# First feed-forward set: lot 5's raw weights in the spare lower-x slot, a lot's rounding ahead of the last lot's lower part, lower weights' products last

## The chip, the cores and the metric

One core of a Trainium2 chip runs the kernel. The metric is the device time of one execution in microseconds (us), lower is better; a measurement is the median of several runs. TensorE (PE), VectorE (DVE), ScalarE (ACT) and GpSimd (POOL) each run their own instruction queue in order; SyncE (SP) issues most DMAs, in order too. They wait for one another by semaphores.

## The reference

Decayed linear attention in blocks, and then a feed-forward layer with squared ReLU, all in float32:

```python
# q, k, v: (4, 8, 768, 64), lam: (8,)
for b in range(S // 64):
    intra = einsum('bhic,bhjc->bhij', qb, kb) * Dmask      # lam ** (i - j), i >= j
    out_b = einsum('bhij,bhjd->bhid', intra, vb) + einsum('bhid,bhde->bhie', qb * lam_pow, kv_state)
    kv_state = lam_block * kv_state + einsum('bhsd,bhse->bhde', kb * rev_pow, vb)
x = out.transpose(0, 2, 1, 3).reshape(3072, 512)
h = maximum(x @ w_in, 0)                                    # w_in: (512, 2048)
y = (h * h) @ w_out                                         # w_out: (2048, 512)
```

## The kernel before

The 3072 tokens are 24 chunks of 128; four chunks make a set of 512 tokens (`N`), and there are six sets. Each float32 product on PE is made as three products of rounded operands: an upper part (`h`) and a lower part (`l`, what the rounding left) of each side, upper by upper, lower by upper, upper by lower. So the weights must stand in SBUF as `wh` and `wl`, and a set's attention result as `xh` and `xl`.

The change lies in the loop over the first set, `for f in range(NF)` at line 1075, 16 iterations. Iteration f computes `hidden(0, f)` (12 matmuls: 128 columns of `w_in`, upper and lower weights, by 512 tokens), squares it on ACT (`square`, three instructions), takes the lower part `gl` on DVE (`rest`), and runs `project(0, f - 1)` (12 matmuls into four accumulators). Beside that, every fourth iteration carries one chunk of attention of the next set: `step = f % 4` tells which piece (scores in step 0, masked scores and the scaled query in step 1, `attend` in step 2, state and lower x in step 3).

The same loop prepares the weights. They are given in float64 and read as pairs of 32-bit words, in 17 lots (`NLOT`); lot u holds block u of `w_in` and block u - 1 of `w_out`, and iteration f needs lot f complete. A lot goes through these steps:

- `wload(u)`: SP issues two DMAs of 512 KB into a tile `raw` (tag "raw", two slots). It is called two iterations ahead of the lot's rounding, and waits until the slot is free.
- `first_hi(u)`, line 120, and `first_lo(u)`, line 125: two ACT passes over `raw`; the first writes a new tile `A` (tag "A", two slots), the second works in place in `raw`.
- `clamp`, `shift`, `sign`, lines 133, 137, 144: three DVE passes over `A`.
- `rounded(u)`, line 150: DVE adds the low word; the last reader of `raw[u]`, whose slot then comes free.
- `upper(u)`, line 156: ACT casts `A` to `wh`.
- `lower(u)`, line 159: DVE writes `A - wh` to `wl`; the last reader of `A`, whose slot then comes free.
- `turn(u)`, line 164: a one-element POOL copy that reads `wl` into `mark`, so that POOL goes on only after `lower`.

In iteration f, `u_ = f + 2`: for f of 3 and more DVE runs clamp, shift and sign of lot u_, then lower of lot u_ - 1, (in step 3 a state update,) then rounded of lot u_, then `gl`. ACT runs first_hi and first_lo of lot u_ + 1 behind the squares, and the cast of lot u_ - 1 ahead of them (in step 2 that of lot u_ behind the passes). POOL runs, behind `turn`, the fading of the state (`fade_state`, line 508) and the scaling of keys (`scale_k`, line 382) in step 0, and of the query (`scale_q`, line 390) in step 1. Iterations 0 to 2 have orders of their own.

The tag "xl" has two slots of the same size as a `raw` tile. One holds the first set's lower x; the other held chunk 3's lent attention operands, whose last reader runs before the loop, and is kept for the second set's lower x, which `attend` starts to write in step 3 of the first four iterations (line 367). A tag's new tile takes a slot that is free in the order of the program. The schedule is by hand: the order of the calls is the order of each queue.

Of the kernel before, what the change touches and what calls it, by code (L numbers as in the profile page):

```python
# [7 lines left out]
F32 = mybir.dt.float32  # L8
F32R = mybir.dt.float32r
U32 = mybir.dt.uint32  # L10
I64 = mybir.dt.int64
AF = mybir.ActivationFunctionType
ALU = mybir.AluOpType
PSUM = bass.MemoryType.PSUM

P = 128
# [5 lines left out]
DM = H * D  # L22
DF = 2048
KT = DM // P
NF = DF // P
G = 4
N = G * C
# [4 lines left out]
NLOT = NF + 1  # L32
# [3 lines left out]
def body(ctx: ExitStack, tc: tile.TileContext, qT, kT, kvq, lam, w, out):  # L36
# [3 lines left out]
    wk = ctx.enter_context(tc.tile_pool(name="wk", bufs=2))  # L40
# [53 lines left out]
    wh = const.tile([P, 2 * NF, DM], F32R, name="wh")  # L94
    wl = const.tile([P, 2 * NF, DM], F32R, name="wl")
# [4 lines left out]
    def lot(t, u):  # L100
        if u in (0, NF):
            return t[:, u : u + 1]
        return t.rearrange("p (s f) d -> p s f d", s=2)[:, :, u]

    def pieces(u):
        return [x for x in ((0, u), (1, u - 1)) if 0 <= x[1] < NF]

    raw, cv = {}, {}

    def wload(u, engine=nc.sync):  # L110
        if u < NLOT:
            x = pieces(u)
            raw[u] = wk.tile([P, len(x) * DM], I64, name="raw", tag="raw")
            for i, (side, f) in enumerate(x):
                engine.dma_start(out=raw[u][:, i * DM : (i + 1) * DM], in_=w[side, :, f])

# [31 lines left out]
    def rounded(u):  # L148
        L, Hw, A = cv[u]
        V.tensor_tensor(out=A, in0=A, in1=L, op=ALU.add)  # L150

    def whole(u):
        return cv[u][2].bitcast(F32).rearrange("p (a d) -> p a d", d=DM)

    def upper(u):
        nc.scalar.copy(lot(wh, u), whole(u))  # L156

    def lower(u):
        V.tensor_tensor(out=lot(wl, u), in0=whole(u), in1=lot(wh, u).bitcast(F32), op=ALU.subtract)  # L159
        cv.pop(u)  # L160
# [15 lines left out]
    def where(x, base, pattern, step, compare, fill):  # L176
# [17 lines left out]
        out=pz[:, C - T : C - T + NX], data0=s[:, 0:1].broadcast_to([P, NX]), data1=spike,  # L194
# [13 lines left out]
    for j in range(2):  # L208
# [5 lines left out]
        lambda o, x, y, op=op: V.tensor_tensor(out=o, in0=x, in1=y, op=op)  # L214
# [5 lines left out]
    b_, t_, u_, c_, d_, af = (sq[:, i, 0 : NS - 1] for i in range(6))  # L220
# [11 lines left out]
    for k in range(NS - 3, NS):  # L232
        n = 1 << k
        V.tensor_scalar(
            out=pz[:, Z + n : Z + 2 * n], in0=pz[:, Z : Z + n], scalar1=tr[:, k : k + 1], scalar2=None,
# [42 lines left out]
    xs_of = {}  # L278
# [81 lines left out]
    def attend(t):  # L360
        KEPT[t] = wk.tile([P, DM], F32, name="kept", tag="a")
        go(t, t + 1, False, scored=False)
        xh, xl = xs_of[t // G]
        cs = slice(t % G * C, (t % G + 1) * C)
        x = KEPT.pop(t).rearrange("p (a b) -> p a b", a=KT)
        nc.scalar.copy(xh[:, :, cs], x)
        return lambda: V.tensor_tensor(
            out=xl[:, :, cs], in0=x, in1=xh[:, :, cs].bitcast(F32), op=ALU.subtract
        )

    part_of = {}
# [71 lines left out]
    def begin(t):  # L443
        begun_of[t] = [ps_a.tile([P, DM], F32, name="att") for _ in range(2)], set()
        old_state(t, 0)

    def begun_mark(t):
        c = (NPR - 1) * D
        nc.scalar.copy(mark[:, 2:3], begun_of[t][0][0][0:1, c : c + 1])

    def go(t, after, apart, mid=None, scored=True):
        if t not in begun_of:
            begin(t)
            begun_mark(t)
        o = u = begun_of[t][0]
        vs = tok[t][1]
        if after is not None and scored:
            scores_by_half(after, ps_h, "h")
            if apart:
                u = sc_of[after]  # L460

        def all_news():
            for p in range(NPR):
                if t % NCB < NCB - 1:
                    news_of(0, t, u[0], p, apart)
                if after is not None:
                    news_of(1, after, u[1], p, apart)

        if apart:
            all_news()  # L470
        old_state(t, 1)
        a = a_of.pop(t)
        for p in range(NPR):
            for h in range(2):
                for j, r in enumerate(rows):
                    add_to(t, h, p, j, vs[rows[h], 2 * p + j, :], a[rows[h], j, p, :], True)
        if not apart:
            all_news()
        if after is not None:
            part_of[after] = u[1]  # L480
            if scored:
                masked_by_half(after)
        if mid is not None:
            mid()
        x = kept(t).rearrange("p (a two c) -> p a two c", two=2, c=C)
        for h in range(2):
            y = o[h][:, 0 : NPR * D].rearrange("p (a two c) -> p a two c", two=2, c=D)
            nc.scalar.copy(x[:, :, 0, of_half(h)], y[:, :, 0])
            for j, r in enumerate(rows):
                nc.scalar.copy(x[r, :, 1, of_half(h)], y[rows[1 - j], :, 1])  # L490
        part_of[t] = u[0]
# [22 lines left out]
    def hidden(m, f, xh, xl):  # L514
        h = ps_h.tile([P, N], F32, name="h")
        k = 0
        for wt, x in ((wh, xh), (wl, xh), (wh, xl)):
            for kt in range(KT):
                nc.tensor.matmul(  # L519
                    h, wt[:, f, kt * P : (kt + 1) * P], x[:, kt], start=k == 0, stop=k == 11  # L520
                )
                k += 1
        return h

    def square(h):
        nc.scalar.activation(h, h, AF.Relu)  # L526
        gh = wk.tile([P, N], F32R, name="gh")
        nc.scalar.activation(gh, h, AF.Square)
        nc.scalar.activation(h, h, AF.Square)  # L529
        return gh  # L530
# [38 lines left out]
                for k in range(i, i + n):  # L569
                    step(k)  # L570

    def new_x(m):
        xs_of[m] = [wk.tile([P, KT, N], F32R, name=n, tag=n) for n in ("xh", "xl")]

# [111 lines left out]
    wt = dram.tile([NF // 2, P, 4, 2, 2 * P], F32, name="wt")  # L688
# [320 lines left out]
    o, u, low = {}, {}, {}  # L1009
# [61 lines left out]
    scale_k(G)  # L1071

    prev = None
    new_x(1)
    for f in range(NF):
        t, step, u_ = G + f // 4, f % 4, f + 2
        h = hidden(0, f, *xs_of[0])
        if step == 2:
            begin(t)
        if f == 2:  # L1080
            gh = square(h)
            begun_mark(t)
            upper(u_ - 1)
        if f < 3:
            if f < 2:
                lower(u_ - 1)
            clamp(u_)
            shift(u_)
            if f == 2:
                lower(u_ - 1)  # L1090
            if f == 1:
                turn(u_, True)
                masked_by_half(t)
                scale_q(t)
                scale_k(t + 1)
                state(t, True)
            sign(u_)
            if f != 1:
                rounded(u_)
        else:  # L1100
            if u_ < NLOT:
                for op in (clamp, shift, sign):
                    op(u_)
            if step < 3:
                upper(u_ - 1)
            lower(u_ - 1)
            if u_ - 1 < NF:
                turn(u_ - 1, False)
            if step == 3:
                state(t, False)  # L1110
            if u_ < NLOT:
                rounded(u_)
        wload(u_ + 2)
        if f == 0:
            fade_state(False)
        if step == 0 and f:
            if t % NCB < NCB - 1:
                fade_state(True)
            scale_k(t + 1)
        if step == 1 and f > 1:  # L1120
            scale_q(t)
        if f != 2:
            gh = square(h)
            if step == 2:
                begun_mark(t)
        rest(0, f, h, gh)
        if step == 3:
            low[t]()
            state(t + 1, True, f == NF - 1)
        if f == 1:  # L1130
            rounded(u_)
        if step == 1 and f > 1:
            masked_by_half(t)
        if f == 0:
            upper(u_)
        if u_ + 1 < NLOT:
            first_hi(u_ + 1)
            first_lo(u_ + 1)
        if step == 2 and u_ < NLOT:
            upper(u_)  # L1140
        if prev is not None:
            project(*prev)
        prev = (0, f)
        if step == 2:
            low[t] = attend(t)
            load_qk(t + 2)
            load_kv(t + 2)
        if f == 0:
            open_half(t)
        elif step == 0:  # L1150
            scores_by_half(t, ps_a, "att")
        if f == NF - 1:
            scores_by_half(t + 1, ps_a, "att")
            scale_k(t + 2)
# [14 lines left out]
    for j, tag in enumerate(("xh", "xl")):  # L1169
        x = wk.tile([P, 4, DM], F32, name="raws", tag=tag)  # L1170
# [14 lines left out]
    for f in range(NF):  # L1185
        t = first_t + f // 2
# [16 lines left out]
        if f == NF - 1:  # L1203
            x = far(*pair(3))
# [4 lines left out]
        if f % 2 == 0:  # L1209
            go(t, t + 1 if t < last_t else None, False)  # L1210
            if t == last_t:
                x = near(*pair(3), "a")
# [16 lines left out]
    m, first_t, last_t = 2, 4 * G, 6 * G - 1  # L1229
# [11 lines left out]
    for f in range(NF):  # L1241
        t = first_t + f // 2
# [97 lines left out]
```

## Time and profile before

| | us |
|---|---|
| median of 3 runs | 585.36 (584.14 to 586.4) |
| the profiled execution | 585.99 |
| its span in the trace | 584.3 |
| PE busy | 572.0 (98%) |
| DVE busy | 415.5 (71%) |
| ACT busy | 278.6 (48%) |
| POOL busy | 101.6 (17%) |

All times below are us from the span's start, in that one execution; the loop over the first set takes from 25.5 to about 124. "Busy" counts instructions only, not waiting. Matmuls are pipelined: one of 512 columns is shown with some 0.39 us, and they follow one another every 0.227. A wait's view tells who waited for whom, and in a timeline a bracket at the end of a line tells how long the engine stood idle just before, and whose end it awaited. The granted TensorE clock is 1.00 in the whole loop.

### The profile page before, as it was taken

To read this page: it belongs to the slowest core of one execution; us is meant where nothing else is said; L and a number is where in the kernel's file an instruction comes from. 1 tells how busy PE (TensorE), PEld (TensorE's weight loads), DVE (VectorE), ACT (ScalarE), POOL (GpSimd) and SP (SyncE) were. 2 spreads that over 40 slices of the span, in tenths; PEclk is the share of its full clock that TensorE was granted. 3 is DMA by queue.
4 is the path that set the end of the run, shared out by engine and by line. 5 is a ranking of instruction groups with operands and counts; after the bars stand their busy time and mean duration, and the time that the engine had idled before them with its cause. 6 is when DMAs were issued, how large, how long until landed. Compare 5 with 4: busy or idle time off the path is not lost.

```text
span 584.3 us, 13118 instructions
## 1 busy us (share of the span) xinstructions
PE 572.0 (98%) x5276; PEld 481.7 (82%) x5276; DVE 415.5 (71%) x685; ACT 278.6 (48%) x529; POOL 101.6 (17%) x110
## 2 busy tenths in 40 slices
PE   9998999999999999999999999999999999999996
PEld 7886787878888887888888887888788888999996
DVE  6898999952678675786666668677645456997933
ACT  4677888844454455433333334445523244641510
POOL 4531322332322231000000003355100000000000
PEclk9999999999999999999999999999999999999999
DMA  8956475424689786466666644632297665767863
GB/s 301 346 170 231 148 256 197 157 75 145 196 277 382 236 272 225 153 191 218 198 199 198 197 163 152 235 124 74 74 315 229 195 194 176 257 213 206 285 204 108
DMA packets 69388, 119.35 MB, mean 204 GB/s; under 512 B 6352, under 2 KB 30928, under 8 KB 69328
## 3 DMA queue, kind: packets, MB, share of 16 engines
q1 hardware_dynamic: 66864, 115.37, 60.7%
q10 hardware_dynamic: 2464, 3.15, 1.5%
q8 instruction: 42, 0.69, 0.4%
q14 instruction: 18, 0.15, 0.1%
HBM read 88.08 MB, written 29.36 MB: 201 GB/s over the span
## 4 chain that ended last, share of the span: by engine, by line
PE 69%; DVE 10%; DMA 9%; ACT 5%; issue 4%; SPq 2%; POOL 1%; DVEq 0%; ACTq 0%; POOLq 0%
PE h L679 19%; PE acc L927 8%; PE att L679 7%; PE acc L549 7%; PE acc L554 6%; PE acc L550 6%; PE h L519 5%; PE att L927 4%; DMA raw<-in_w 3%; PE att L429 2%; PE h L927 2%; DMA kv_sb<-in_kvq 2%; DVE A L144 2%; DMA ws<-parts 2%; DMA lent<-in_qT 1%
## 5 line engine op out<-in xcount | busy, mean ns | idle before, releaser
L549 PE MATMUL acc<-wh,gh 128*128 128x512 f32 x256 | 101.2, 395 | 0.0
L554 PE MATMUL acc<-wh,gl 128*128 128x512 f32 x256 | 100.0, 390 | 0.1
L550 PE MATMUL acc<-wl,gh 128*128 128x512 f32 x256 | 99.7, 389 | 0.0
L679 PE MATMUL h<-wh,ring 128*128 128x512 f32 x320 | 85.8, 390 | 0.1
L526 ACT ACTIVATE h<-h 128x512 f32<-128x512 f32 x48 | 27.9, 582 | 94.8 <-PE h L519 37.0
L679 PEld LDWEIGHTS h<-wh,ring 128*128 128x128 f32 x320 | 59.9, 188 | 13.2 <-issue 0.5
L534 DVE TENSOR_TENSOR gl<-h,gh 128x512 fp32r<-128x512 f32 x48 | 33.0, 688 | 40.1 <-ACT h L529 40.1
L554 PEld LDWEIGHTS acc<-wh,gl 128*128 128x128 f32 x256 | 48.0, 188 | 11.0 <-DVE gl L534 0.9
L549 PEld LDWEIGHTS acc<-wh,gh 128*128 128x128 f32 x256 | 48.0, 188 | 10.4
L550 PEld LDWEIGHTS acc<-wl,gh 128*128 128x128 f32 x256 | 48.1, 188 | 9.7
L679 PE MATMUL h<-wl,ring 128*128 128x512 f32 x160 | 49.3, 389 | 0.0
L508 POOL TENSOR_TENSOR kvd<-kv,qpow 128x256 f32<-128x256 f32 x33 | 28.9, 874 | 85.2 <-DVE kv L214 74.5
L382 POOL TENSOR_TENSOR kv_sb<-kv_sb,mask 128x512 f32<-128x512 f32 x17 | 20.9, 1227 | 125.1 <-DMA kv_sb<-in_kvq 123.4
L519 PE MATMUL h<-xh,wh 128*128 128x512 f32 x128 | 36.7, 408 | 1.4 <-ACT wh L156 1.0
L519 PE MATMUL h<-xh,wl 128*128 128x512 f32 x128 | 34.8, 394 | 1.1 <-DVE wl L159 1.0
L927 PE MATMUL acc<-folds,wh 128*128 128x256 f32 x192 | 35.2, 283 | 0.0
L679 PEld LDWEIGHTS h<-wl,ring 128*128 128x128 f32 x160 | 30.0, 188 | 6.3
L519 PE MATMUL h<-xl,wh 128*128 128x512 f32 x128 | 34.3, 390 | 0.0
L679 PE MATMUL att<-wh,ring 128*128 128x512 f32 x128 | 34.2, 389 | 0.0
L214 DVE TENSOR_TENSOR wl<-sums,wh 128x1024 fp32r<-128x1024 f32 x24 | 29.3, 1219 | 1.8 <-ACT wh L899 1.8
L519 PEld LDWEIGHTS h<-xh,wl 128*128 128x128 f32 x128 | 23.8, 188 | 7.5 <-DVE wl L159 2.4
L927 PEld LDWEIGHTS acc<-folds,wh 128*128 128x128 f32 x192 | 30.0, 192 | 0.0
(249 smaller groups left out, 1189.6 us busy)
## 6 DMA issues: line engine op xcount, KB each, us to landing
ring<-ws SPq DMA_DIRECT2D x112, 256.0 KB, 3.0
folds<-wt SPq DMA_DIRECT2D x64, 256.0 KB, 3.7
raw<-in_w SPq DMA_DIRECT2D x30, 512.0 KB, 4.4
kv_sb<-in_kvq SPq DMA_DIRECT2D x19, 512.0 KB, 5.5
ws<-parts SPq DMA_DIRECT2D x32, 256.0 KB, 4.7
qk_sb<-in_kT SPq DMA_DIRECT2D x20, 256.0 KB, 4.6
qk_sb<-in_qT SPq DMA_DIRECT2D x20, 256.0 KB, 4.5
out_x<-o SPq DMA_DIRECT2D x16, 256.0 KB, 4.7
```

The costliest lines, as they stand in the source:

```text
L144: V.scalar_tensor_tensor(out=A, in0=Hw, scalar=0xC0000000, in1=A, op0=ALU.bitwise_and, op1=ALU.bitwise_or)
L214: lambda o, x, y, op=op: V.tensor_tensor(out=o, in0=x, in1=y, op=op)
L382: nc.gpsimd.tensor_tensor(out=x, in0=x, in1=y.broadcast_to([P, NPR, 2, D]), op=ALU.mult)
L508: nc.gpsimd.tensor_tensor(out=kvd, in0=d, in1=qpow[:, :, D - 1 : D].broadcast_to([P, NPR, D]), op=ALU.mult)
L519: nc.tensor.matmul(h, wt[:, f, kt * P : (kt + 1) * P], x[:, kt], start=k == 0, stop=k == 11)
L526: nc.scalar.activation(h, h, AF.Relu)
L534: V.tensor_tensor(out=gl, in0=r, in1=gh.bitcast(F32), op=ALU.subtract)
L549: nc.tensor.matmul(accs[m][i], gh[:, cs], wh[:, j], start=f == 0, stop=False)
L550: nc.tensor.matmul(accs[m][i], gh[:, cs], wl[:, j], start=False, stop=False)
L554: nc.tensor.matmul(accs[m][i], gl[:, cs], wh[:, j], start=False, stop=end)
L679: nc.tensor.matmul(bank, x[:, part_, kt], t[:, q + kt], start=start and z == 0, stop=stop and z == 5, skip_group_check=True,)
L927: nc.tensor.matmul(bank[:, r * 2 * P : (r + 1) * 2 * P], x, y, start=n == 0 and r == 0 and z == 0, stop=n == NQ - 1 and z == 2, skip_group ...
```

## The change

`wload` takes lot 5's tile from the tag "xl" and not from "raw". The second set's lower x is therefore made later: `new_x(1, False)` makes the upper one alone, and `new_low(1)` the lower one in iteration 3, behind the rounding of lot 5; `attend` looks the lower tile up only when it writes. From iteration 3 on, `rounded(u_)` is called right behind `sign(u_)`, ahead of `lower(u_ - 1)`, `turn` and the state update. In `hidden` of the first set, for f of 1 and more, the four products of the lower weights come last, behind those of the lower x.

```diff
@@ -110,7 +110,7 @@
     def wload(u, engine=nc.sync):
         if u < NLOT:
             x = pieces(u)
-            raw[u] = wk.tile([P, len(x) * DM], I64, name="raw", tag="raw")
+            raw[u] = wk.tile([P, len(x) * DM], I64, name="raw", tag="xl" if u == G + 1 else "raw")
             for i, (side, f) in enumerate(x):
                 engine.dma_start(out=raw[u][:, i * DM : (i + 1) * DM], in_=w[side, :, f])
 
@@ -360,12 +360,12 @@
     def attend(t):
         KEPT[t] = wk.tile([P, DM], F32, name="kept", tag="a")
         go(t, t + 1, False, scored=False)
-        xh, xl = xs_of[t // G]
+        xh = xs_of[t // G][0]
         cs = slice(t % G * C, (t % G + 1) * C)
         x = KEPT.pop(t).rearrange("p (a b) -> p a b", a=KT)
         nc.scalar.copy(xh[:, :, cs], x)
         return lambda: V.tensor_tensor(
-            out=xl[:, :, cs], in0=x, in1=xh[:, :, cs].bitcast(F32), op=ALU.subtract
+            out=xs_of[t // G][1][:, :, cs], in0=x, in1=xh[:, :, cs].bitcast(F32), op=ALU.subtract
         )
 
     part_of = {}
@@ -514,7 +514,10 @@
     def hidden(m, f, xh, xl):
         h = ps_h.tile([P, N], F32, name="h")
         k = 0
-        for wt, x in ((wh, xh), (wl, xh), (wh, xl)):
+        order = ((wh, xh), (wl, xh), (wh, xl))
+        if m == 0 and f:
+            order = order[0], order[2], order[1]
+        for wt, x in order:
             for kt in range(KT):
                 nc.tensor.matmul(
                     h, wt[:, f, kt * P : (kt + 1) * P], x[:, kt], start=k == 0, stop=k == 11
@@ -569,8 +572,11 @@
                 for k in range(i, i + n):
                     step(k)
 
-    def new_x(m):
-        xs_of[m] = [wk.tile([P, KT, N], F32R, name=n, tag=n) for n in ("xh", "xl")]
+    def new_x(m, low=True):
+        xs_of[m] = [wk.tile([P, KT, N], F32R, name=n, tag=n) for n in ("xh", "xl")[: 1 + low]]
+
+    def new_low(m):
+        xs_of[m].append(wk.tile([P, KT, N], F32R, name="xl", tag="xl"))
 
 
 
@@ -1071,7 +1077,7 @@
     scale_k(G)
 
     prev = None
-    new_x(1)
+    new_x(1, False)
     for f in range(NF):
         t, step, u_ = G + f // 4, f % 4, f + 2
         h = hidden(0, f, *xs_of[0])
@@ -1103,13 +1109,15 @@
                     op(u_)
             if step < 3:
                 upper(u_ - 1)
+            if u_ < NLOT:
+                rounded(u_)
+            if f == 3:
+                new_low(1)
             lower(u_ - 1)
             if u_ - 1 < NF:
                 turn(u_ - 1, False)
             if step == 3:
                 state(t, False)
-            if u_ < NLOT:
-                rounded(u_)
         wload(u_ + 2)
         if f == 0:
             fade_state(False)
```

## Rows read from the trace of the kernel before

**Rows 1.** Busy time: length; PE, PEld, DVE, ACT, POOL; clock, DMA share, GB/s.

```profile
60.00:80.00 20.00, 19.58 (x157) 15.43 (x156) 19.32 (x24) 16.84 (x27) 5.26 (x5) 1.00 0.67 218
```

**Rows 2.** Waits of PE, 24 to 125: waiter, releaser, us, times, longest.

```profile
PE h L519 <- DVE wl L159: 1.0, 2, 0.7
PE h L519 <- ACT wh L156: 1.0, 1, 1.0
PE att L429 <- ACT mark L449: 0.5, 1, 0.5
PE att L429 <- POOL qk_sb L390: 0.3, 1, 0.3
```

**Rows 3.** Timeline of ACT: start, us, line, operation, tiles, count, [idle before, releaser].

```profile
46.39 1.14 ACT L120 ACTIVATE A<-raw 128x1024 f32<-128x1024 f32 x1 [4.68 <-DMA raw<-in_w]
48.48 1.03 ACT L156 CAST wh<-A 128x1024 fp32r<-128x1024 f32 x1
```

**Rows 4.** Timeline of PE: hidden(0,4), its first and its lower weights' products.

```profile
49.55 1.21 PE L519 MATMUL h<-xh,wh 128*128 128x512 f32 x4 [0.97 <-ACT wh L156]
51.43 1.19 PE L519 MATMUL h<-xh,wl 128*128 128x512 f32 x4 [0.66 <-DVE wl L159]
```

**Rows 5.** Timeline of DVE: lower(3), sign(4), rounded(4), lower(4).

```profile
41.75 1.23 DVE L159 TENSOR_TENSOR wl<-A,wh 128x1024 fp32r<-128x1024 f32 x1
42.89 1.22 DVE L144 SCALAR_TENSOR_TENSOR A<-raw,A 128x1024 uint32<-128x1024 uint32 x1
44.14 1.23 DVE L150 CUSTOM_DVE_ANT_0 A<-raw,A 128x2048 uint16<-128x2048 uint16 x1
...
50.16 1.22 DVE L159 TENSOR_TENSOR wl<-A,wh 128x1024 fp32r<-128x1024 f32 x1
```

**Rows 6.** SP at line 115, 31.5 to 32.5 (lot 4): issues, landing.

```profile
L115 SPq DMA_DIRECT2D raw<-in_w x2: 328/377/426, 31.8 to 32.2; - x2
DMA to landing us min/median/max: 3.7/4.2/4.6
```

**Rows 7.** The same, 45.7 to 46.3 (lot 6; q, k, v behind): landing.

```profile
DMA to landing us min/median/max: 3.8/4.2/4.6
```

**Rows 8.** Timeline of DVE in iteration 6: clamp, sign, lower, rounding, gl.

```profile
66.86 0.69 DVE L133 TENSOR_SCALAR A<-A 128x1024 f32<-128x1024 f32 x1
...
68.31 1.23 DVE L144 SCALAR_TENSOR_TENSOR A<-raw,A 128x1024 uint32<-128x1024 uint32 x1
69.45 1.22 DVE L159 TENSOR_TENSOR wl<-A,wh 128x1024 fp32r<-128x1024 f32 x1
70.59 1.22 DVE L150 CUSTOM_DVE_ANT_0 A<-raw,A 128x2048 uint16<-128x2048 uint16 x1
71.72 0.69 DVE L534 TENSOR_TENSOR gl<-h,gh 128x512 fp32r<-128x512 f32 x1
```

**Rows 9.** Waits of ACT from 24 to 125, its first passes.

```profile
ACT A L120 <- DMA raw<-in_w: 10.6, 7, 4.7
ACT A L120 <- DVE wl L159: 4.0, 4, 1.4
```

**Rows 10.** Timeline of POOL: marks at line 164, and a scaling of keys.

```profile
51.51 0.17 POOL L164 COPY mark<-wl 1x1 f32<-1x1 f32 x1 [10.98 <-DVE wl L159]
...
64.68 1.04 POOL L164 COPY mark<-wl 1x1 f32<-1x1 f32 x1 [3.81 <-DVE wl L159]
...
110.21 1.05 POOL L382 TENSOR_TENSOR kv_sb<-kv_sb,mask 128x512 f32<-128x512 f32 x1
```

**Rows 11.** Timeline of DVE: the clamp of lot 15.

```profile
110.15 1.67 DVE L133 TENSOR_SCALAR A<-A 128x1024 f32<-128x1024 f32 x1
```

**Rows 12.** Timeline of PE: first products of hidden(0,9), (0,10), (0,13).

```profile
83.43 1.19 PE L519 MATMUL h<-xh,wh 128*128 128x512 f32 x4
...
89.00 1.08 PE L519 MATMUL h<-xh,wh 128*128 128x512 f32 x4
...
108.81 1.19 PE L519 MATMUL h<-xh,wh 128*128 128x512 f32 x4
```

## The prediction

> **What bounds the kernel now.** I read the busy time of each engine by stretch first, then the waits of TensorE (PE), then those of ScalarE (ACT), then the timelines around the largest wait. In the loop that the change touches (25 to 122 us; after it PE again has no large waits) PE is busy in nearly all of each stretch, and VectorE (DVE) almost as much [rows 1]: 19.6 and 19.3 of 20 us. PE sets the pace and DVE is just behind it. All that PE visibly waits for in the loop comes to 2.8 us: 1.0 for an upper weight part, 1.0 for lower parts, 0.5 for the mark, 0.3 for the scaled query [rows 2]. The view counts a wait from a modelled end, about 0.16 us after the next matmul could have started, and short gaps around these add a little; so some 4.3 us is all that can be won here, 0.7% of the time.
>
> The largest waits are lot 5's. ACT stands 4.68 us for its raw weights and starts on them at 46.39; only behind its two passes, at 48.48, comes the cast of lot 4's upper part [rows 3]. So PE starts hidden(0,4) at 49.55 after a wait, and stands again until lot 4's lower part is there, at 51.43 [rows 4]. DVE writes that lower part from 50.16 [rows 5].
>
> **Part 1: lot 5's raw weights in the empty lower x.** Before, lot 5 has the slot of lot 3, which comes free when lot 3 is rounded, near 40. The spare xl slot last held chunk 3's lent operands, whose last matmuls run before the loop. So SP, which issues lot 4 at 31.8 and 32.2 [rows 6], issues lot 5 right behind, at about 33. Lot 4 took up to 4.6 us to land; lot 5, with that megabyte ahead of it, should land at 38 to 40 and not at 46.3. This takes no instruction away. Does it hold up lot 4? Lot 6 was issued with a chunk's q, k and v (1 MB as well) right behind on the same queue, and landed in 3.8 and 4.6 us [rows 7], as lot 4 did with nothing behind it: cost 0. The Trainium skill, "DMA: Bandwidth & Descriptors", section "Issuing engines are not separate DMA queues", says that DMAs share the same 16 engines and interleave. Read as sharing between neighbours this would make lot 4 late; [rows 6, 7] do not show that, and I keep it as rival C.
>
> SP is moved too: lots 6 and 7 now take the slots of lots 3 and 4 and are issued one iteration earlier, and chunk 6's loads, queued behind lot 6, go out near 43 instead of 46. Nobody waits for those; value 0.
>
> What is next? The rounding buffer A has two slots, so lot 5's first pass needs lot 3's lower part written; DVE starts that at 41.75 and it takes 1.23 [rows 5]. So ACT runs the passes of lot 5 from 43.0 to 45.3, and the upper cast of lot 4 when lot 4 is rounded (44.14 + 1.23 = 45.4 [rows 5]), ready at 46.4 and not 49.5. hidden(0,4) then starts when PE is free, 1.1 us earlier. DVE need not wait for lot 5 any more and comes to clamp(5) at 45.9 (rounding 1.14 and gl 0.60 behind 44.14). After clamp, shift, sign and rounding (clamp and shift 1.45 and rounding 1.14, from starts in [rows 8]; sign 1.25, from 42.89 to 44.14 in [rows 5], since the rounding right behind must await its result: 0.1 more than before a lower) it reaches lot 4's lower part at 49.7 and ends it at 50.9. Thanks to part 3 PE needs it only 8 matmuls into hidden(0,4), at about 50.3: it waits 0.7, less than the 0.97 that now passes there. With the small gaps behind it PE is 2.0 us ahead at hidden(0,5).
>
> **Part 2: rounding ahead of the lower part.** Per iteration from f = 3 on, rounding (1.14 by starts) moves ahead of lower. It frees the raw slot 1.14 us earlier, and the upper cast can run earlier, but lower(u-1) is 1.2 us later, and three things hang on it.
>
> First, PE's lower weights: paid back by part 3 with 4 matmuls, 0.91 us. Second, the POOL mark and, queued behind it, the query and key scaling. The mark took 1.04 us beside a rounding and 0.17 beside another instruction (64.68 and 51.51) [rows 10]; it now falls beside gl, so POOL gets back 0.9 of the 1.2. Third, and dearest, ACT's first pass of lot u+1: it takes the A slot that lower(u-1) frees, and already waits for just that in 4 iterations, 4.0 us in all [rows 9]. The pass takes 1.14 [rows 3]. Today DVE meanwhile rounds (1.14) and makes gl (0.60) [rows 8], and finds the pass done. After the change it has gl alone. In a plain iteration (steps 0 and 2) DVE's round becomes clamp and shift 1.45 + sign 1.25 + rounding 1.14 + lower 1.22 + pass 1.14 and 0.08 for two handovers (0.03 of it seen between 42.89 + 1.22 and 44.14 in [rows 5]) = 6.28, against 5.46 today (66.86 to 71.72, plus 0.60) and 5.57 that PE takes (83.43 to 89.00 [rows 12]). In step 1 the masked scores (some 0.7) fill the hole, also 6.28. In step 3 low and state fill it: about 6.9, plus some 0.5 of waiting for ACT's squares. Four iterations: 3 x 6.28 + 7.4 = 26.2. In f = 8 and f = 12 POOL's fading and scaling now run right behind the mark, and the clamp comes while they hold the port: a clamp beside such an instruction took 1.67 [rows 11] and not 0.69 [rows 8], and ended 0.56 after POOL's (110.21 + 1.05 [rows 10]). POOL ends at lower + 1.9 and the clamp thus at lower + 2.45 and not 1.9: 0.5 more, 26.7 in all. PE took 25.38 from 83.43 to 108.81 [rows 12]. So DVE, with the A slots, becomes the pace: +1.3 per four iterations.
>
> **Part 3: lower weights' products last.** No instruction more or less; the lower x of set 0 is complete before f = 1. It moves PE's need of the lower weights by 0.91 us. Counted above.
>
> **The sum.** Lead at hidden(0,5): -2.0. Cycle f = 5 to 8: this one has no fading at f = 4, starts with the lead, and today already runs slow for DVE's sake: +0.4 (waits of about 0.65, 0.8 and 0.6 at the lower parts of 5 and 6 and at the query, for 0.6, 0.25 and 0.5). Cycle 9 to 12: +1.3, most at the lower part of lot 10. f = 13 and 14: the plain iterations 12 and 14 and the port again, +1.4, most at the lower part of lot 14. Together +1.1. Other end: the small gaps of today's loop, about 0.1 at each change of tile shape, lie under the new waits or beside them; if beside, up to +2.3. I take +1.5, nearer the end that is counted from the trace's own starts. PE is the pace after the loop, so it reaches the end whole. The profiled execution took 585.99 us (span 584.3, the rest lies around it), 0.6 above the median 585.36, inside the runs' spread. 585.99 + 1.5 = 587.5; against the median, 586.9.
>
> **The rivals.**
> A, forecast: the A slots eat the lead and a little more, 585.4 to 588.5. Chance 0.50.
> B, the lead stays: if PE's gaps rather than DVE set the rounds, or ACT's pass lies under gl and the late clamp costs PE nothing, -2.0 to -2.6 remain: 582.5 to 583.5; the most, with all 4.3 won, 581. For it: today DVE has about 1 us spare in four iterations, and 10.6 us of ACT's waits are for loads that now come earlier [rows 9]. Against it: 6.28 against 5.57. Chance 0.20.
> C, lot 5's load slows lot 4's: by [rows 6, 7] not; if lot 4 lands 1.2 later, ACT's mark comes 1.2 later, of which about 0.5 is slack, and PE stands 0.7 more: 587.6. Chance 0.05. The Trainium skill's sentence on interleaving is this case.
> D, slower: the mechanism of the forecast with the port. If POOL holds the port at the clamp in most iterations, and not only at f = 8 and 12, such an iteration costs 0.5 more and none catches up: four of them beyond the counted ones, 2.0, make +3.5 with the forecast's 1.5: 588.9. It decides from the point at which POOL is still busy when the clamp may start, 1.2 us behind lower, in steps 1 and 2 too. Chance 0.20.
> E, it does not do what it says: lot 5 still starts its passes after 46 (another holder of the slot or of A): no lead, but the price of part 2: about +3.1 (1.1 and the lead of 2.0), 588.5. The slot's last user is long done, which speaks against it; chance 0.05.
>
> **How the numbers follow.** The forecast is A: 586.9. 583.0 to 589.2 leaves out part of B at the low end and the tails of D and E, under 0.2. About 0.5% (2.9 us) is what a measurement of this kernel tells from no change: faster than 582.4 is only the better half of B, 0.10; slower than 588.3 is D, most of E and little of A, 0.23; the rest 0.67.
>
> **What would show it.** Lot 5's first pass at about 43 and PE's wait at hidden(0,4)'s upper part gone (part 1); the POOL mark at about 0.2 us in most iterations; ACT's first pass waiting for the lower part in nearly every iteration and not for a DMA; DVE idle about 0.6 to 0.7 before the clamps of lots 7, 9, 11, 13 and 15; PE waiting about 1.2 for the lower parts of lots 10 and 14 (part 2). If those clamps start without a wait, my round of 6.28 is wrong and it is B.

## The result

The changed kernel took 588.99 us (median of 4 runs, 588.7 to 589.49) against 585.12 of before in the same session: ratio 1.0066, 95% interval [1.0045, 1.0087], 3.9 us slower. Its profiled execution took 589.0 (span 587.3), that of before 585.99 (584.3): 3.0 between the two, since the profiled run of before lay 0.9 above its median. With four runs on each side the interval is wide: 2.6 to 5.1 us slower. In the larger groups timed later, before took 585.95 and 585.76, so the true distance may be nearer 3 than 4.

Where in the loop it went shows in the starts of `hidden(0, f)` on PE. Of the changed kernel (from `hidden` on, line numbers shift by 3; its matmuls are at line 522), from two stretches of PE's timeline (start, us, line, operation, tiles):

```profile
48.33 1.07 PE L522 MATMUL h<-xh,wh 128*128 128x512 f32 x4
...
55.46 1.19 PE L522 MATMUL h<-xh,wh 128*128 128x512 f32 x4
...
82.38 1.19 PE L522 MATMUL h<-xh,wh 128*128 128x512 f32 x4
```

```profile
109.47 1.19 PE L522 MATMUL h<-xh,wh 128*128 128x512 f32 x4
...
124.87 1.19 PE L522 MATMUL h<-xh,wh 128*128 128x512 f32 x4
```

Of before, the two that [rows 4, 12] do not have:

```profile
57.20 1.19 PE L519 MATMUL h<-xh,wh 128*128 128x512 f32 x4
...
122.10 1.19 PE L519 MATMUL h<-xh,wh 128*128 128x512 f32 x4
```

| hidden(0, f) starts | f = 4 | f = 5 | f = 9 | f = 13 | f = 15 |
|---|---|---|---|---|---|
| before | 49.55 | 57.20 | 83.43 | 108.81 | 122.10 |
| after | 48.33 | 55.46 | 82.38 | 109.47 | 124.87 |
| difference | -1.22 | -1.74 | -1.05 | +0.66 | +2.77 |

So the lead of part 1 is there, 1.74 us at f = 5, and is lost again at a growing rate: +0.69 over four iterations, +1.71 over the next four, +2.11 over the last two. From there the distance stays: at the second set's last blocks, near 230 us, it is still 2.74.

The lead first. ACT's first passes over lots 4 and 5 in the changed kernel, DVE's lower part of lot 3, and SP's four issues of lots 4 and 5 with their landings; the last line is the landing of lot 4's two alone:

```profile
36.52 1.14 ACT L120 ACTIVATE A<-raw 128x1024 f32<-128x1024 f32 x1
...
42.93 1.15 ACT L120 ACTIVATE A<-raw 128x1024 f32<-128x1024 f32 x1 [1.61 <-issue]
```

```profile
41.63 1.22 DVE L159 TENSOR_TENSOR wl<-A,wh 128x1024 fp32r<-128x1024 f32 x1
```

```profile
L115 SPq DMA_DIRECT2D raw<-in_w x4: 328/401/430, 31.7 to 33.1; - x4
DMA to landing us min/median/max: 3.4/5.1/6.8
```

```profile
DMA to landing us min/median/max: 3.4/3.9/4.3
```

The pass over lot 5 starts at 42.93 where [rows 3] had 46.39; the load is there by 40 (issued until 33.1, landing within 6.8), and what the pass now waits for is lot 3's lower part, as reckoned. The bracket names no releaser, but the lower part ends at 42.85 (41.63 + 1.22), 0.08 ahead of the pass. PE's wait for lot 4's upper part is gone. What replaced it is PE's new list of waits in the loop, 24 to 128 us (waiter, releaser, us in total, times, longest), and that of ACT's first pass, both to be held against [rows 2, 9]:

```profile
PE h L522 <- DVE wl L159: 4.3, 6, 1.2
PE att L429 <- POOL qk_sb L390: 0.7, 2, 0.4
PE att L429 <- ACT mark L449: 0.3, 1, 0.3
```

```profile
ACT A L120 <- DVE wl L159: 16.9, 9, 2.3
```

```profile
DVE A L133 <- ACT A L120: 3.0, 5, 0.6
```

PE waits 4.3 us for lower weights, not 1.0. ACT's first pass waits for the lower part in 9 iterations, 16.9 us, and no longer for any load; and DVE, which is to clamp what that pass writes, stands 5 times for it. DVE's timeline in iterations 5 to 7 shows the mechanism (a bracket at the end is the idle time before and its releaser):

```profile
59.16 0.70 DVE L133 TENSOR_SCALAR A<-A 128x1024 f32<-128x1024 f32 x1 [0.62 <-ACT A L120]
59.88 0.69 DVE L137 TENSOR_SCALAR A<-A 128x1024 uint32<-128x1024 uint32 x1
60.61 1.23 DVE L144 SCALAR_TENSOR_TENSOR A<-raw,A 128x1024 uint32<-128x1024 uint32 x1
61.98 1.23 DVE L150 CUSTOM_DVE_ANT_0 A<-raw,A 128x2048 uint16<-128x2048 uint16 x1
63.12 1.22 DVE L159 TENSOR_TENSOR wl<-A,wh 128x1024 fp32r<-128x1024 f32 x1
64.25 0.68 DVE L537 TENSOR_TENSOR gl<-h,gh 128x512 fp32r<-128x512 f32 x1
64.86 0.74 DVE L214 TENSOR_TENSOR a<-att,mask 128x256 f32<-128x256 f32 x2
65.55 0.90 DVE L133 TENSOR_SCALAR A<-A 128x1024 f32<-128x1024 f32 x1
...
67.22 1.23 DVE L144 SCALAR_TENSOR_TENSOR A<-raw,A 128x1024 uint32<-128x1024 uint32 x1
68.58 1.23 DVE L150 CUSTOM_DVE_ANT_0 A<-raw,A 128x2048 uint16<-128x2048 uint16 x1
69.72 1.22 DVE L159 TENSOR_TENSOR wl<-A,wh 128x1024 fp32r<-128x1024 f32 x1
70.86 0.68 DVE L537 TENSOR_TENSOR gl<-h,gh 128x512 fp32r<-128x512 f32 x1
72.14 0.69 DVE L133 TENSOR_SCALAR A<-A 128x1024 f32<-128x1024 f32 x1 [0.60 <-ACT A L120]
```

and ACT's pass between the last two:

```profile
70.97 1.14 ACT L120 ACTIVATE A<-raw 128x1024 f32<-128x1024 f32 x1 [1.79 <-DVE wl L159]
```

Lines 133, 137, 144 are clamp, shift and sign, 150 the rounding, 159 the lower part, 537 `gl`. Set it beside [rows 8]: lower now starts behind the rounding (69.72), `gl` follows, and then DVE stands 0.60 us until ACT's pass over the next lot, which could start only when lower ended (69.72 + 1.22 = 70.94), is through. From clamp to clamp iteration 6 takes 6.59 us (65.55 to 72.14), 5.46 before; 0.2 of it is the longer clamp at 65.55. Iteration 5, with masked scores behind `gl`, takes 6.39. A second, smaller cost stands in the same lines: from sign to the next instruction it is 1.36 to 1.37 (60.61 to 61.98, 67.22 to 68.58), where with lower behind sign it was 1.14 (68.31 to 69.45 in [rows 8]). So in every iteration in which it is moved the rounding costs DVE 0.23 us more, and where `gl` alone stands behind lower the hole of 0.6 comes on top.

### The profile page after: what moved, and what is told of

Same layout as the page of the kernel before. It is cut to its first block, busy times and chain, and to the rows that moved or that the text cites. A ratio compares the mean times of both kernels' runs of the same rounds, so it can differ in the third digit from the quotient of the medians.

```text
span 587.3 us, 13123 instructions
## 1 busy us (share of the span) xinstructions
PE 573.3 (98%) x5276; PEld 482.1 (82%) x5276; DVE 416.7 (71%) x685; ACT 278.5 (47%) x529; POOL 93.4 (16%) x110
## 4 chain that ended last, share of the span: by engine, by line
PE 71%; DVE 14%; ACT 6%; issue 4%; DMA 3%; SPq 1%; POOL 0%; DVEq 0%; ACTq 0%; POOLq 0%
PE h L685 19%; PE acc L933 7%; PE att L685 7%; PE acc L552 6%; PE acc L557 6%; PE acc L553 6%; PE h L522 5%; PE att L933 4%; PE att L429 2%; DVE A L144 2%; PE h L933 2%; DVE wl L159 2%; DMA ws<-parts 2%; DVE A L133 1%; DVE sums L214 1%
## 5 line engine op out<-in xcount | busy, mean ns | idle before, releaser
L508 POOL TENSOR_TENSOR kvd<-kv,qpow 128x256 f32<-128x256 f32 x33 | 27.0, 819 | 85.0 <-DVE kv L214 68.0
```

What stands on the lines that cost most here:

```text
L508: nc.gpsimd.tensor_tensor(out=kvd, in0=d, in1=qpow[:, :, D - 1 : D].broadcast_to([P, NPR, D]), op=ALU.mult)
```

## The experiments

Two theories. **A-slot**: rounding ahead of lower puts ACT's first pass into DVE's own round, because the pass needs the A slot that lower frees; DVE's round grows past PE's. **Lateness**: the round matters little, the lower weights simply come 1.2 us later in it, and PE stands for them. They agree on nearly everything in the trace of the change, so each run touches what only one of them cares for. Times are medians; before was timed beside each group of kernels (585.12 beside the change, 585.95 beside the first four below it, 585.76 beside the last three), and the ratios are what is compared.

| kernel | us | ratio to before, 95% interval | us to before |
|---|---|---|---|
| the change | 588.99 | 1.0066 [1.0045, 1.0087] | +3.9 |
| slot_order: rounding put back | 583.43 | 0.9955 [0.9942, 0.9968] | -2.6 |
| round_alone | 590.52 | 1.0078 [1.0066, 1.0090] | +4.6 |
| slot_round: without part 3 | 589.18 | 1.0058 [1.0046, 1.0070] | +3.4 |
| halves | 587.24 | 1.0026 [1.0015, 1.0037] | +1.5 |
| round_odd | 584.59 | 0.9979 [0.9966, 0.9992] | -1.2 |
| round_even | 587.49 | 1.0032 [1.0021, 1.0043] | +1.9 |
| slot_alone | 584.03 | 0.9973 [0.9963, 0.9984] | -1.6 |

(The last column is the ratio times 585.9, less that.)

**slot_order**, the change with one part undone:

```diff
-            if u_ < NLOT:
-                rounded(u_)
-            if f == 3:
-                new_low(1)
             lower(u_ - 1)
 ...
             if step == 3:
                 state(t, False)
+            if u_ < NLOT:
+                rounded(u_)
+            if f == 3:
+                new_low(1)
```

> The change with the rounding put back behind the lower part; lot 5's slot and the lower weights' products last stay. Theory A-slot (rounding ahead of lower makes ACT's first pass, which needs the A slot that lower frees, stand in DVE's own round, so DVE becomes the pace): no hole before the clamps, lot 5 starts its passes at about 43, PE keeps the lead of some 2.0 to 2.4 us: 582.5 to 583.3 beside 585.1 of before. Theory lateness (the only harm is that the lower weights come 1.2 us later for PE): the same, 582.5 to 583.3. Rival that the slot itself is harmful (loads collide, other queues): no gain, 585 or more.

583.43, the fastest of all here and faster than before beyond its interval. The slot and the order of the products are thus worth 2.6 us, and the moved rounding takes that and some 3 to 4 more. DVE stands for ACT's pass once in the loop, 0.4 before lot 10's clamp, and not five times. Its timeline shows the clamp of lot 8 right behind its predecessors, with no idle time (start, us, line; `gl`, masked scores, clamp; and the clamp of lot 9):

```profile
63.30 0.68 DVE L537 TENSOR_TENSOR gl<-h,gh 128x512 fp32r<-128x512 f32 x1
63.91 0.74 DVE L214 TENSOR_TENSOR a<-att,mask 128x256 f32<-128x256 f32 x2
64.57 0.68 DVE L133 TENSOR_SCALAR A<-A 128x1024 f32<-128x1024 f32 x1
...
69.43 0.68 DVE L537 TENSOR_TENSOR gl<-h,gh 128x512 fp32r<-128x512 f32 x1
70.03 0.68 DVE L133 TENSOR_SCALAR A<-A 128x1024 f32<-128x1024 f32 x1
```

From clamp to clamp it is 5.46 us here (64.57 to 70.03) and 6.59 in the change. The rival that the slot itself does harm is out; A-slot and lateness expected the same of this run.

**round_alone**, before with the moved rounding only:

```diff
+            if u_ < NLOT:
+                rounded(u_)
             lower(u_ - 1)
 ...
-            if u_ < NLOT:
-                rounded(u_)
```

> Before, with rounding ahead of the lower part from iteration 3 on, and nothing else. A-slot: rounds of DVE of about 6.4 us in steps 0, 1 and 2 as in the change, and no lead to pay from: 5 to 6 us slower than before, about 590.5. Lateness: 2 to 4 us slower from PE's waits, with DVE's rounds as before where PE does not hold them. Rival that the moved rounding is free and the loss is the slot's: no difference to before.

590.52, 4.6 us over before (3.9 to 5.3 by the interval): between what lateness gave (2 to 4) and what A-slot gave (5 to 6), and no verdict by itself. But the hole before the clamps is the change's, here lot 7's, with lower and `gl` ahead of it:

```profile
58.11 1.22 DVE L159 TENSOR_TENSOR wl<-A,wh 128x1024 fp32r<-128x1024 f32 x1
59.25 0.68 DVE L534 TENSOR_TENSOR gl<-h,gh 128x512 fp32r<-128x512 f32 x1
60.54 0.69 DVE L133 TENSOR_SCALAR A<-A 128x1024 f32<-128x1024 f32 x1 [0.61 <-ACT A L120]
```

**slot_round**, the change with the lower weights' products back in the middle of every `hidden`:

```diff
-        order = ((wh, xh), (wl, xh), (wh, xl))
-        if m == 0 and f:
-            order = order[0], order[2], order[1]
-        for wt, x in order:
+        for wt, x in ((wh, xh), (wl, xh), (wh, xl)):
```

> The change without its third part: lower weights' products stay in the middle in every iteration. A-slot: DVE's round sets the pace and does not care when within hidden PE stands; only the phase moves, once, by at most 0.9 us, and PE then stands longer at fewer places: 0 to 0.9 us slower than the change, 589.0 to 589.9. Lateness: each of the change's six waits for lower weights grows by up to 0.9 us, 3 to 5 us more: 592 to 594.

589.18: within the intervals, no different from the change. PE now needs the lower weights 0.91 us sooner in every iteration, and the times show no cost of it; in the trace `hidden(0, 15)` starts 0.5 later (125.38 and not 124.87), a shift that is there once. PE's waits for them, 24 to 128 us:

```profile
PE h L519 <- DVE wl L159: 6.2, 7, 1.6
```

They grow from 4.3 to 6.2, but the waits for the query and the mark that the change has beside them are gone from the list: PE stands at another place in the same round, whose length DVE sets. Lateness alone called for 592 to 594; it is out as the main cause.

**halves**, the change with the handover cut in two, over the same two A buffers (allocated once, so that each half is followed by itself):

```diff
-        A = wk.tile([P, r.shape[1]], U32, name="A")
-        nc.scalar.activation(A.bitcast(F32), r[:, :, 1].bitcast(F32), AF.Abs)
+        if not A2:
+            A2.extend(wk.tile([P, 2 * DM], U32, name="A") for _ in range(2))
+        A = A2[u % 2][:, 0 : r.shape[1]]
+        for x in range(0, r.shape[1], DM):
+            nc.scalar.activation(A[:, x : x + DM].bitcast(F32), r[:, x : x + DM, 1].bitcast(F32), AF.Abs)
 ...
-        V.tensor_tensor(out=lot(wl, u), in0=whole(u), in1=lot(wh, u).bitcast(F32), op=ALU.subtract)
+        l, w_, h_ = lot(wl, u), whole(u), lot(wh, u).bitcast(F32)
+        for x in range(w_.shape[1]):
+            V.tensor_tensor(out=l[:, x], in0=w_[:, x], in1=h_[:, x], op=ALU.subtract)
```

> The change, with the first pass and the lower part each made in two halves over the same two A buffers, so that the pass over the first half can follow lower's first half. Costs DVE about 0.08 and ACT about 0.1 us per iteration. A-slot: the hole before the clamp falls from 0.6 to about 0.25 us, plain rounds from 6.4 to some 6.1: 1.2 to 2 us faster than the change, about 587.3. Lateness: lower's end comes 0.08 later, no gain: 589 to 589.6. Port rival (POOL's instructions at the clamp): no gain, or 0.3 less loss at two clamps.

587.24: 2.4 us of the loss come back by the ratios, 1.75 by the medians and 1.8 by the traced spans (587.3 and 585.5), though DVE has more instructions than in the change and lower ends no sooner in its round (5.23 behind the clamp of lot 6, 5.17 in the change). Lower (two halves merged in one line), `gl` and the clamp of lot 7, and the clamps of lots 8 and 9:

```profile
57.00 1.29 DVE L164 TENSOR_TENSOR wl<-A,wh 128x512 fp32r<-128x512 f32 x2
58.21 0.68 DVE L542 TENSOR_TENSOR gl<-h,gh 128x512 fp32r<-128x512 f32 x1
59.03 0.87 DVE L136 TENSOR_SCALAR A<-A 128x1024 f32<-128x1024 f32 x1
...
65.63 0.68 DVE L136 TENSOR_SCALAR A<-A 128x1024 f32<-128x1024 f32 x1
...
71.61 0.69 DVE L136 TENSOR_SCALAR A<-A 128x1024 f32<-128x1024 f32 x1
```

`gl` hands on after 0.60 where the next instruction need not wait (69.43 to 70.03 above), so the hole is 0.2 and not 0.6. A plain round is 5.98 (65.63 to 71.61), where the change takes 6.37 to 6.39. This is the run that only A-slot explains: neither the order of DVE's work nor what PE asks for is touched.

**round_odd** and **round_even**, the change with rounding ahead of lower in half of the steps only:

```diff
+            if step % 2:        # round_odd; round_even: step % 2 == 0
             (rounding ahead of lower, as in the change)
+            else:
+                (rounding behind, as before)
```

> The change with rounding ahead of lower only in iterations of steps 1 and 3, where masked scores, or state and lower x, fill the time of ACT's pass; in steps 0 and 2 rounding is back behind. A-slot: no hole before any clamp; what is left of the price is the handover to the rounding, 0.1 per such iteration, and the later lower weights, so most of the lead stays: 0.5 to 1.5 us faster than before, 584.4 to 585.4 beside 585.9. Lateness: half of the price stays, 1 us slower than before and more. Port theory: as A-slot here, since the clamps beside POOL's work follow steps 0.

> The reverse: rounding ahead of lower only in steps 0 and 2, where gl alone stands behind lower. A-slot: the holes of 0.6 before the clamps of lots 7, 9, 11, 13, 15 are all there, most of the price too: 1.5 to 2.5 us slower than before, 587.4 to 588.4. Lateness: the same as rounding ahead in steps 1 and 3.

584.59 and 587.49. In steps 1 and 3, where the masked scores, or state and lower x, stand between lower and the next clamp, the move costs 1.4 us of slot_order's lead; in steps 0 and 2, where `gl` alone stands there, 4.5. Each has six of the twelve moved roundings. Lateness has no reason for that difference: PE waits less for lower weights in the slower of the two (1.6 us in round_even, 2.5 in round_odd, 24 to 128 us). Clamps that run beside a POOL instruction are no reason either: those of lots 7, 11 and 15 take 1.09, 1.68 and 1.67 in round_odd and 0.69, 1.26 and 1.23 in round_even. In round_even DVE stands for the pass as often and as long as in the change, in round_odd once, before lot 10's clamp, and there ACT's pass had waited for a load and not for a slot (its timeline, last):

```profile
DVE A L133 <- ACT A L120: 3.0, 5, 0.6
```

```profile
DVE A L133 <- ACT A L120: 1.0, 1, 1.0
```

```profile
77.63 1.12 ACT L120 ACTIVATE A<-raw 128x1024 f32<-128x1024 f32 x1 [1.46 <-DMA raw<-in_w]
```

What the move costs without a hole shows in round_odd's sign and rounding of lot 7, 1.37 from start to start:

```profile
60.22 1.23 DVE L144 SCALAR_TENSOR_TENSOR A<-raw,A 128x1024 uint32<-128x1024 uint32 x1
61.59 1.23 DVE L150 CUSTOM_DVE_ANT_0 A<-raw,A 128x2048 uint16<-128x2048 uint16 x1
```

Its rounds of step 1 take 6.80, 7.38 and 7.34 us, where those of slot_order take 6.53, 7.20 and 7.11: 0.2 to 0.3 more each, about the 0.23 of the sign. Six times 0.23 is 1.4; the hole for the late load (1.0, where slot_order has 0.4) may have a part in it too.

**slot_alone**, part 1 by itself (with the second set's lower x made in iteration 3, as part 1 needs it; those lines are left out here):

```diff
-            raw[u] = wk.tile([P, len(x) * DM], I64, name="raw", tag="raw")
+            raw[u] = wk.tile([P, len(x) * DM], I64, name="raw", tag="xl" if u == G + 1 else "raw")
 ...
```

> Before with lot 5's raw weights in the spare slot, nothing else (the second set's lower x is made in iteration 3). A-slot and lateness: the lead alone, 2.0 to 2.6 us faster than before, 583.3 to 583.9; it differs from the kernel with part 3 as well by no more than 0.4, since with rounding behind lower PE seldom waits for lower weights. If part 3 were what wins, no gain or a small one.

584.03, 1.6 us faster than before, a little short of the 2.0 to 2.6 expected. Its interval and slot_order's overlap, so what part 3 is worth beside it is not settled by the times: 1.0 us by the ratios, where at most 0.4 was expected. Their traces show no gain in the loop: from `hidden(0, 0)` to `hidden(0, 15)` it is 94.39 us in slot_order, 94.21 in slot_alone and 96.58 in before.

A third A slot, which should take the pass out of the round altogether, was not tried.

## Why the prediction was right, and where it was short

**Part 1** came as forecast: load behind lot 4's, landing by 40, pass at 42.93 (forecast 43.0), PE's first wait gone, lead at hidden(0,5) 1.74 (forecast 2.0). It is worth 1.6 by itself (slot_alone), and 2.6 together with part 3 (slot_order). Rival C did not occur: lot 4 landed in 3.4 and 4.3 us with lot 5 right behind it, and ACT began its pass at 36.52, with no idle time before it; the reading of the Trainium skill's sentence on interleaving ("DMA: Bandwidth & Descriptors", "Issuing engines are not separate DMA queues") as a delay for the load ahead is not borne out, as [rows 6, 7] had said.

**Part 2** is what decided, by the mechanism that the prediction named: the pass behind lower in DVE's round, idle time of 0.59 to 0.62 before the clamps of lots 7, 9, 11, 13 and 15 (forecast 0.6 to 0.7), and PE's longest waits at the lower parts of lots 10 and 14, 1.21 and 1.20 (forecast about 1.2):

```profile
91.62 1.21 PE L522 MATMUL h<-xh,wl 128*128 128x512 f32 x4 [1.21 <-DVE wl L159]
...
118.62 1.20 PE L522 MATMUL h<-xh,wl 128*128 128x512 f32 x4 [1.20 <-DVE wl L159]
```

The POOL mark fell to 0.17 everywhere, as forecast (line 164, 45 to 120 us: count, ns min/median/max, first and last start):

```profile
L164 POOL COPY mark<-wl x11: 173/174/176, 51.1 to 118.7; 1x1 f32<-1x1 f32 x11
```

The forecast was 1.5 us slower, the result 3.9 (3.0 between the two traced executions), inside the range of 583.0 to 589.2 but near its end. It is above rival A's own 585.4 to 588.5 and beside D's 588.9, so that the range held is in part luck: its upper end was room left for D, and D's mechanism is not what happened (its clamps, below). E, 588.5, is out by the pass at 42.93.

By the starts of `hidden` the miss adds up: the lead was 0.26 short and the three cycles 0.29, 0.41 and 0.71 longer than forecast, 1.67 on top of +1.1. The terms that were too small:

- **The round of DVE**: 6.28 was reckoned, 6.37 to 6.39 is what one takes where no clamp runs beside POOL (59.16 to 65.55). Sign to rounding took 1.25 by [rows 5] and takes 1.36 to 1.37 in the changed kernel. The DVE queue there holds a separate wait ahead of the rounding, which before has not in that stretch (line 150, 40 to 118 us):

```profile
L150 DVEq EVENT_SEMAPHORE  x11: 21/21/21, 48.5 to 116.1; - x11
```

  The twelfth, of lot 16, comes at 121.6. Twelve times 0.11 is 1.3 us of DVE's time; if it reaches PE whole, which no run shows, it is most of the miss of 1.67. The trace of before could have told: iteration 0 has such a wait (the only one, line 150, 20 to 128 us), and 1.37 from sign to rounding:

```profile
29.20 1.23 DVE L144 SCALAR_TENSOR_TENSOR A<-raw,A 128x1024 uint32<-128x1024 uint32 x1
30.57 1.23 DVE L150 CUSTOM_DVE_ANT_0 A<-raw,A 128x2048 uint16<-128x2048 uint16 x1
```

```profile
L150 DVEq EVENT_SEMAPHORE  x1: 21/21/21, 30.5 to 30.5; - x1
```

  The pair in [rows 5] was taken from iteration 2, where lower stood ahead of both and no separate wait is seen. The reason, by the order of the program: the rounding reads what ACT's second pass leaves. From iteration 2 of before on, the lower part ahead of it waits for a cast that ACT makes later than that pass, so the rounding needs no wait of its own. In iteration 0 the cast came first (25.18, the pass at 27.95), and the wait is there. The wait and the 0.11 go together wherever, in the loop of both traces, a full rounding stands right behind its sign; no run takes the wait away by itself.

  Of the 4.75 us that DVE takes more than in slot_order from the clamp of lot 5 to that of lot 16 (73.99 and 69.24), the holes are 2.6 (3.0 less 0.4), and eleven times 0.23 would be 2.5, together a little more than the whole. So the hole that the prediction named is about half of the price, and the rounding that now stands right behind its sign is about as much; the prediction had 0.11 of the 0.23. This is an estimate from rows, not an experiment of its own.
- **Clamps beside POOL** (the prediction's port): two clamps longer by 0.5 were counted, and came (1.25 and 1.24 us at 85.83 and 112.84). The clamp of lot 8, beside the query's scaling, took 0.90 (65.55 above) and that of lot 16 0.67, where before had 0.41; the prediction had these as rival D and left them out of the sum. They are 0.2 to 0.3 each, not D's four times 0.5, and the clamps of lots 9, 12 and 13 took 0.69.
- **The sum by cycles**: +0.4, +1.3 and +1.4 were forecast, +0.69, +1.71 and +2.11 measured. The last stretch holds the wait for lot 14's lower part (1.20) and behind it one of 0.37 for the query, where before had neither, and the 0.4 by which hidden(0,14) was late already. With the lead of 1.74 it makes +2.77 and not +1.1. This is more than even the other end that the prediction gave this sum, 2.3.
- The rest, 0.2 after the loop in the spans and 0.9 between the profiled run and the median of before, is within what runs of one kernel differ (584.14 to 586.4 for before).

**Part 3** was counted as paying back 0.91 of the 1.2 us by which a lower part comes later. In slot_round no gain of it shows beside part 2: DVE's round sets the pace, and a later deadline on PE does not shorten it.

Rival B (the lead stays) is what the kernel would have been without part 2: slot_order, at 2.6, the upper end of B's 2.0 to 2.6.

## What to carry to other kernels

A step that frees a buffer belongs in its engine's queue as early as the next user needs it, not as late as its own reader allows: with two slots, whatever runs between "last reader done" and "next writer's result needed" is the cover of the writer's time, and moving 1.1 us of work out of that stretch put 0.6 us of idling, and 0.23 of a dearer handover, into a round that had 0.1 us to spare (5.46 beside PE's 5.57). So before reordering an engine that runs close to the pace, list for each moved instruction what stands between the release and the next need, step by step of the loop, and move it only where that still covers the other engine's pass. Ask also what the moved instruction now stands right behind, and look in the trace for a place where that order is there already: here iteration 0 of before had it. Taking a load off the critical slot was a clean gain by itself; it was hidden here by the second edit in the same change.

## What the runs showed of the hardware that was not expected

An order of instructions can carry a wait for free: a rounding behind an instruction that already waited for the same engine had no separate wait, and the same rounding one place earlier got one. From the start of sign to the start of the next instruction the traces show three steps: 1.14 us with lower behind it, 1.25 with the rounding, which needs sign's result, and 1.36 to 1.37 with the rounding and the separate wait.

Cutting an ACT pass and a DVE subtraction of 1024 elements into halves cost little: ACT's two halves took 1.27 together against 1.15, DVE's two 1.29 against 1.22, while the overlap gained 0.4 of the hole of 0.6.
